# First product of an MLP behind an mLSTM cell: contraction of 320 rows in two full 128-row tiles and one 64-row pair, instead of five 64-row pairs

## Chip, core and metric

One core of a Trainium2 chip. The metric is the device time of one execution in microseconds. Before: median 490.5 us of 3 runs (490.28 to 491.42).

## What is computed

An mLSTM cell over 4 batches, 8 heads, 768 steps and head dimension 40, and a two-layer product with a leaky ReLU on its output, all in float32 (the weights `w_in` and `w_out` arrive as float64 and are narrowed on the chip):

```python
# per step t: C = f*C + i*(v k^T), n = f*n + i*k, with stabilised gates
h_tilde = C @ q;  denom = max(|n . q|, 1)
y = sigmoid(o_gate) * h_tilde / denom          # (4, 8, 768, 40)
x = y.transpose(0, 2, 1, 3).reshape(3072, 320) # heads side by side
h = x @ w_in                                   # 3072 x 320 x 2048, the first product
g = maximum(0.01 * h, h)
out = g @ w_out                                # 3072 x 2048 x 320
```

## The kernel before

The sequence is cut into six groups of 128 steps. A step `s` of the kernel is one batch of one group, so a group has four steps. For each step the cell is computed in chunked form by TensorE and DVE: scores (L593, L650), states (L608, L655), values (L673, L713, L743). The first group (steps 0 to 3) has a form of its own, the second another (`u_plain`), and steps from 8 on a third (`u_mix`).

The result of a step, `x` (128 tokens by 320), has to stand with its 320 columns on partitions before the first product can contract over them. For steps 0 to 7 DVE gates the values (`gate`, L685, or L724), GpSimd scales them by the denominators (`scale_x`, L702), TensorE transposes (`u_x`, L876 and L877) and ScalarE copies PSUM to `xT` (`x_copy`, L889 and L890). For later steps the transposed result goes through DRAM (`x_dr`, L762) and is gathered into `xT` by two requests of SyncE's queue (`gather_x`, L773).

The first product of a group, for its 512 tokens at once, makes 16 tiles of 128 hidden columns, two at a time (`j` = 0 to 7). The 320 contraction rows are five slots of 64. TensorE's array is split into two row tiles of 64 rows: row tile `r` = 0 works on one hidden tile and `r` = 1 on the other, beside each other, and both need all 64-row slots of `x`, so `xT` holds `x` twice, once on partitions 0 to 63 and once on 64 to 127, in 5 x 128 columns a step. `w_in` is held as four quarters of 512 hidden columns; on partitions 0 to 63 are the columns of `r` = 0, on 64 to 127 those of `r` = 1. Which row of `w_in` goes to which partition is free as long as `x` follows it.

Three kinds of first product exist. The first group runs in halves of 256 tokens (`half`), groups 1 to 3 in pairs of units of 512 (`pair`), both in fp32 (L907). Groups 4 and 5 split every operand into a rough part and rests and make three fp32r products (`three_units`, L833: "raw" and "low" into `ph`, "dif" into `pe`), which ScalarE and DVE join (L853, L855, L859). The splitting is done by DVE on `w_in` (in halves of 640 columns) and on `xT` (`split_x`, 640 columns a step). The second product follows in each group: plain in the first (L942, 128x320) and in seven block products afterwards (L983, 128x160).

`w_in` is loaded early by SyncE's queue (`load_weights`, "lw 0" to "lw 3" in the order below), ten requests a quarter (L230), each of 64 partitions by 256 float64. "nw" steps narrow a quarter to float32: ScalarE first (L260), then DVE (L262 to L277).

The order of work on PE, DVE, ScalarE and GpSimd is written out by hand, and each engine and queue takes its own in that order. For the first group it is a list (`ORDER`), of which these lines matter; afterwards units of products are interleaved with cell units by tables of places.

```python
ld 0; warm 12; ld 1; ld 2; lo 0; lo 1; lo 2; lw 0
g 0; ld 3; lw 1; lw 2; lo 3; ge 0; ug 0; tr 0 0
x 1; xc 1; gate 2; st 3; o 3; gp 2; nw 1; nw 1
stc 3; nw 1; ff 0; val 3; den 3; x 2; gate 3; fd 4
```

Here "ld" and "lo" are loads, "x" the transpose, "xc" the copy, "st" the state (L608), "ff" a unit of the first product. PSUM is two pools of four banks: `psf` ("mm") for the products, `psc` ("c") for cell work, transposes and `pe`.

Of the kernel before, what the change touches and what calls it, by code (L numbers as in the profile page):

```python
# [22 lines left out]
def kernel(  # L23
# [181 lines left out]
    def load_weights(n):  # L205

        m = n - QN
        if n < QN:
            dst = w_in[:, n, :]
        else:  # L210
            dst = w_out[:, 2 * m : 2 * m + 2, :].rearrange("p a d -> p (a d)")
        to = dst
        if wide:
            if n < 2:
                at = NF * GT - 2 * WC * (n + 1)
                raw = acts_l[:, at : at + 2 * WC].bitcast(U64)
            elif n < QN:
                raw = raw_t[:, WC * (n - 2) : WC * (n - 1)]
            elif m < 2:
                raw = w_out[:].rearrange("p f d -> p (f d)")[:, (2 + m) * WC : (3 + m) * WC].bitcast(U64)  # L220
            else:
                at = (4, 0, 1, 2, 3, 4)[m - 2] * HW
                raw = raw_t[:, at : at + HW]
            raws[n] = (raw, dst)
            to = raw
        if n < QN:
            src = moe_w_in[:, n * QC : (n + 1) * QC].rearrange("(p k) (r c) -> r p k c", p=DP, r=2)
            for slot in range(KC):
                for r in range(2):
                    nc.sync.dma_start(  # L230
                        to[DP * r : DP * (r + 1), 2 * P * slot : 2 * P * (slot + 1)], src[r, :, slot, :],
                    )
# [448 lines left out]
    def gate(s):  # L681

        d = st[s]
        d["x"] = cw.tile([P, Dm], F32, name="x")
        nc.vector.scalar_tensor_tensor(  # L685
            x_by(d["x"], H), in0=d["o"].rearrange("p (h a k) -> p h a k", h=H, k=KC), scalar=1.0,
            in1=d["pa"][:, :, :D].rearrange("p h (a k) -> p h a k", k=KC), op0=ALU.add, op1=ALU.mult,
        )

    def gate_scale(s):  # L690

        scale_x(st[s]["x"], st[s]["den"])

    def x_by(x, m):

        return x[:].rearrange("p (k m a) -> p m a k", k=KC, m=m)

    def scale_x(x, den):

        x4 = x[:].rearrange("p (k h a) -> p k h a", k=KC, h=H)  # L700
        by = den[:].unsqueeze(1).unsqueeze(3).to_broadcast([P, KC, H, DP // H])
        nc.gpsimd.tensor_tensor(x4, x4, by, op=ALU.mult)  # L702

    def u_plain(s):

        c, b = divmod(s, B)
        d = st[s]
        prep_o(s)
        hN = psc.tile([P, H, 2, V1], F32, name="hN", tag="c")
        m = mixed(s)  # L710
        for h in range(H):
            for u in range(2):
                nc.tensor.matmul(  # L713
                    hN[ts(u, SL), h].rearrange("p k d -> p (k d)"), lhsT=m[:, u, h, :], rhs=S_v[s % NL][:, u, h, :, :V1],
                    start=True, stop=True,
                )
        state_next(s, 1)
        den = cw.tile([P, H], F32, name="den")
        denominators(den[:], hN[:, :, 0, DB])
        if b < 2:  # L720
            d["x"] = cw.tile([P, Dm], F32, name="x")[:]
        else:
            d["x"] = wk.tile([P, H, D1], F32, name="hn")[:].rearrange("p h d -> p (h d)")[:, :Dm]
        nc.vector.scalar_tensor_tensor(  # L724
            x_by(d["x"], 2 * H), in0=natural(s, 2).rearrange("p h (k a i) -> p (h k) a i", k=2, i=KC), scalar=1.0,
            in1=hN[:].rearrange("p h k d -> p (h k) d")[:, :, :DB].rearrange("p n (a i) -> p n a i", i=KC),
            op0=ALU.add, op1=ALU.mult,
        )
        scale_x(d["x"], den)
        state_add(s, 1)  # L730

    def u_mix(s):
# [32 lines left out]
    def gather_x(s):  # L765

        c, b = divmod(s, B)
        if ("xT", c) not in st:
            st["xT", c] = wk.tile([P, B, KC * P], F32R if c in THREE else F32, name="xT", bufs=1)
        xT = st["xT", c][:].bitcast(F32)  # L770
        src = x_dr[s].rearrange("(m w) t -> m w t", w=QW)[:, :DB, :].rearrange("m (a k) t -> m a (k t)", k=KC)
# [7 lines left out]
    def open_parts():  # L779

        cells_stack.close()
        kp = ctx.enter_context(tc.tile_pool(name="kp", bufs=1))
        for key in ("raw", "low", "dif"):
            parts["w", key] = [kp.tile([P, WC], F32R, name=f"w_{key}{n}") for n in range(QN)]
        for key in ("low", "dif"):
            parts["x", key] = kp.tile([P, B, KC * P], F32R, name=f"x_{key}")
        parts["tmp"] = [kp.tile([P, KC * P], F32, name=f"tmp{n}") for n in range(2)]
        parts["n"] = 0

    def tmp_part():  # L790
# [10 lines left out]

    def split(src, low, dif):

        t = tmp_part()[:]
# [18 lines left out]
    def three_units(g, lead):  # L823

        xs = {"raw": by_slot(st["xT", g], F32R), "low": by_slot(parts["x", "low"], F32R), "dif": by_slot(parts["x", "dif"], F32R)}

        def rows(j, ph, key, start, stop):
            n, e = divmod(j, 2)
            for slot in range(KC):
                at = (2 * slot + e) * P  # L830
                for r in range(2):
                    part = slice(DP * r, DP * (r + 1))
                    nc.tensor.matmul(  # L833
                        ph[r][:], lhsT=parts["w", key][n][part, at : at + P], rhs=xs[key][part, slot, :],
                        start=start and slot == 0, stop=stop and slot == KC - 1,
                    )

        def triple(j):
            ph, pe = [], []

            def first():
                ph.extend(psf.tile([P, GT], F32, name=f"ph{r}", tag="mm") for r in range(2))
                rows(j, ph, "raw", True, False)

            def second():
                rows(j, ph, "low", False, True)

            def third():
                pe.extend(psc.tile([P, GT], F32, name=f"pe{r}", tag="c") for r in range(2))
                rows(j, pe, "dif", True, True)  # L850
# [19 lines left out]
    def u_x(s):  # L870

        c, b = divmod(s, B)
        d = st[s]
        xt = st["xt", s] = psc.tile([P, KF + 1, P], F32, name="xt", tag="c")
        for kk in range(KF):
            nc.tensor.transpose(xt[:, kk, :], d["x"][:, ts(kk, P)], ident[:])  # L876
        nc.tensor.transpose(xt[:KR, KF, :], d["x"][:, KF * P :], ident[:])  # L877
        del st[s]

    def x_copy(s):  # L880

        c, b = divmod(s, B)
        if b == 0:
            st["xT", c] = wk.tile([P, B, KC * P], F32, name="xT", bufs=1)
        xt = st.pop(("xt", s))
        xT = st["xT", c][:, b, :].rearrange("p (k t) -> p k t", t=P)
        for r in range(2):
            rows = ts(r, DP)
            nc.scalar.copy(xT[rows, 0::2, :], xt[:DP])  # L889
            nc.scalar.copy(xT[rows, 1::2, :], xt[DP:, :KF])  # L890

    def u_x1(s):
        u_x(s)
# [6 lines left out]
    def ff_units(g):  # L900
        xT = by_slot(st["xT", g])

        def rows(j, ph, cols, slots):
            bs = slice(cols.start // P, cols.stop // P)
            for slot in slots:
                for r in range(2):
                    nc.tensor.matmul(  # L907
                        ph[r][:, cols], lhsT=w_row(r, slot, j), rhs=xT[DP * r : DP * (r + 1), slot, bs, :],
                        start=(slot == 0), stop=(slot == KC - 1),
                    )  # L910

        def relu(j, ph, cols):
            for r in range(2):
# [3 lines left out]
        def pair(j):  # L917
            ph = []

            def first():  # L920
                ph.extend(psf.tile([P, GT], F32, name=f"ph{r}", tag="mm") for r in range(2))
                rows(j, ph, slice(0, GT), range(3))

            def second():
                rows(j, ph, slice(0, GT), range(3, KC))
                relu(j, ph, slice(0, GT))

            return [first, second]
# [1 line left out]
        def half(j, h):  # L930
            ph = [psf.tile([P, GT], F32, name=f"ph{r}", tag="mm") for r in range(2)]
            cols = slice(h * GT // 2, (h + 1) * GT // 2)
            rows(j, ph, cols, range(KC))
            relu(j, ph, cols)

        po = {}
# [393 lines left out]
```

## Time and profile before

| | |
|---|---|
| median of the runs | 490.5 us |
| profiled execution, span | 489.4 us |
| rest between the two | 1.1 us |
| TensorE busy | 476.1 us |
| first product, fp32 (L907) | 800 records, 146.3 us |
| first product, fp32r (L833) | 480 records, 63.4 us |
| second product (L942, L983) | 1248 records, 194.8 us |
| granted TensorE clock, mean | 0.982 |

Read the page's busy times for the engines, then the chain of work that ended last, then the waits of PE. An fp32 matmul stands in the trace as two records (two passes), an fp32r matmul as one. In a name such as "64*128" the first number is the rows and the second the columns of the array in use. Two records of row tiles that run beside each other overlap, so a group's busy time is smaller than its count times the mean. DMA requests that are being issued stand under "SPq".

### The profile page before, as it was taken

To read this page: it belongs to the slowest core of one execution; us is meant where nothing else is said; L and a number is where in the kernel's file an instruction comes from. 1 tells how busy PE (TensorE), PEld (TensorE's weight loads), DVE (VectorE), ACT (ScalarE), POOL (GpSimd) and SP (SyncE) were. 2 spreads that over 40 slices of the span, in tenths; PEclk is the share of its full clock that TensorE was granted. 3 is DMA by queue.
4 is the path that set the end of the run, shared out by engine and by line. 5 is a ranking of instruction groups with operands and counts; after the bars stand their busy time and mean duration, and the time that the engine had idled before them with its cause. 6 is when DMAs were issued, how large, how long until landed. Compare 5 with 4: busy or idle time off the path is not lost.

```text
span 489.4 us, 12856 instructions
## 1 busy us (share of the span) xinstructions
PE 476.1 (97%) x5137; PEld 377.9 (77%) x5137; DVE 365.9 (75%) x595; ACT 197.4 (40%) x510; POOL 160.3 (33%) x207
## 2 busy tenths in 40 slices
PE   7969998999999999999999999999999999999997
PEld 6857887777745479975559995557998889988997
DVE  5796999799924999777898777679899968335611
ACT  4674885453642240324342141425024752156310
POOL 4234454070600725817280563644220002100020
PEclk9867999999999999999999999999999999999999
DMA  7777686898623566668787877755151030100001
GB/s 136 177 191 146 161 226 134 216 229 177 143 97 90 133 158 176 162 152 202 152 197 160 189 181 177 184 144 153 44 229 42 1 107 1 42 15 0 1 1 54
DMA packets 142699, 63.41 MB, mean 130 GB/s; under 512 B 110832, under 2 KB 130864, under 8 KB 142640
## 3 DMA queue, kind: packets, MB, share of 16 engines
q1 hardware_dynamic: 142256, 62.47, 52.7%
q8 instruction: 40, 0.66, 0.6%
q14 instruction: 19, 0.16, 0.1%
q10 hardware_dynamic: 384, 0.13, 0.1%
HBM read 51.68 MB, written 8.27 MB: 122 GB/s over the span
## 4 chain that ended last, share of the span: by engine, by line
PE 82%; SPq 8%; DVE 5%; issue 2%; DMA 2%; ACT 1%; ACTq 0%; DVEq 0%
PE po L983 32%; PE ph L907 24%; PE ph L833 8%; PE po L942 6%; PE pe L833 4%; PE pT L743 3%; PE sd L650 3%; SPq L230 3%; SPq L368 2%; SPq L377 1%; PE sd L655 1%; DVE w_in L275 1%; PE hN L713 1%; DMA raw<-in_moe_w_in_dram 1%; DVE late L266 1%
## 5 line engine op out<-in xcount | busy, mean ns | idle before, releaser
L907 PE MATMUL ph<-xT,w_in 64*128 64x512 f32 (+1 forms) x800 | 146.3, 516 | 0.2 <-ACT xT L889 0.2
L907 PEld LDWEIGHTS ph<-xT,w_in 64*128 64x128 f32 x800 | 77.8, 190 | 57.4 <-issue 50.8
L983 PE MATMUL po<-w_out,acts 128*128 128x160 f32 x640 | 91.0, 301 | 0.0
L983 PEld LDWEIGHTS po<-w_out,acts 128*128 128x128 f32 x640 | 87.5, 190 | 3.4 <-ACT w L488 1.5
L915 ACT ACTIVATE acts<-ph 128x512 f32<-128x512 f32 (+1 forms) x80 | 36.8, 508 | 83.6 <-PE ph L907 83.5
L488 ACT ACTIVATE w<-w,gT 128x64 f32<-128x64 f32 (+1 forms) x192 | 52.0, 349 | 29.0 <-POOL w L480 28.0
L628 POOL TENSOR_TENSOR S<-S,f 40x336 f32<-40x336 f32 x36 | 32.5, 902 | 93.3 <-PE pT L743 49.5
L983 PE MATMUL po<-raw,acts 128*128 128x160 f32 x320 | 45.1, 299 | 0.0
L983 PEld LDWEIGHTS po<-raw,acts 128*128 128x128 f32 x320 | 44.0, 190 | 0.0
L660 DVE TENSOR_TENSOR qn<-w,sd 64x512 f32<-64x512 f32 x40 | 27.4, 684 | 21.0 <-PE sd L655 14.0
L1016 POOL TENSOR_TENSOR y<-y,raw 128x160 f32<-128x160 f32 x10 | 5.5, 555 | 112.3 <-ACT y L1015 112.3
L942 PE MATMUL po<-w_out,acts 128*128 128x320 f32 x128 | 36.0, 436 | 0.0
L855 DVE SCALAR_TENSOR_TENSOR acts<-ph,acts 128x512 f32<-128x512 f32 x32 | 20.6, 684 | 20.7 <-ACT acts L853 20.7
L541 DVE TENSOR_TENSOR qn<-kqT,late 64x512 f32<-64x512 f32 x32 | 33.1, 1033 | 1.0
L480 POOL TENSOR_TENSOR w<-w,i 128x512 f32<-128x512 f32 x20 | 31.8, 1591 | 2.7 <-ACT acts L915 1.9
L942 PEld LDWEIGHTS po<-w_out,acts 128*128 128x128 f32 x128 | 23.8, 190 | 9.5 <-issue 0.3
L757 POOL TENSOR_TENSOR xb<-xb,den 128x320 f32<-128x320 f32 x16 | 11.6, 727 | 48.7 <-DVE xb L754 48.7
L853 ACT ACTIVATE acts<-pe 128x512 f32<-128x512 f32 x32 | 17.4, 594 | 19.2 <-PE pe L833 19.0
L761 DVE STREAM_TRANSPOSE x<-xb 128x512 f32<-128x512 f32 x16 | 17.8, 1114 | 7.7 <-POOL xb L757 7.7
L859 ACT ACTIVATE acts<-acts 128x512 f32<-128x512 f32 x32 | 19.7, 633 | 8.0 <-DVE acts L855 8.0
L983 PE MATMUL po<-raw 128*128 128x160 f32 x160 | 22.7, 300 | 0.0
L650 PEld LDWEIGHTS sd<-kqT 40*64 40x64 f32 x640 | 19.7, 135 | 3.7 <-issue 3.0
(166 smaller groups left out, 773.2 us busy)
## 6 DMA issues: line engine op xcount, KB each, us to landing
w<-a_dr SPq DMA_DIRECT2D x40, 128.0 KB, 3.7
rb<-in_k_dram SPq DMA_DIRECT2D x64, 80.0 KB, 3.1
rb<-in_q_dram SPq DMA_DIRECT2D x64, 80.0 KB, 2.7
rb<-in_o_gate_dram SPq DMA_DIRECT2D x64, 80.0 KB, 2.6
xT<-x_dr SPq DMA_DIRECT2D x32, 160.0 KB, 3.2
late<-a_dr SPq DMA_DIRECT2D x32, 128.0 KB, 3.4
x_dr<-x SPq DMA_DIRECT2D x16, 256.0 KB, 3.4
kn<-in_k_dram SPq DMA_DIRECT2D x24, 160.0 KB, 3.7
```

Of the source, the lines that this page charges most:

```text
L480: nc.gpsimd.tensor_tensor(w, w, cm2.unsqueeze(1).to_broadcast([P, H, SL]), op=ALU.add)
L488: yield nc.scalar.activation(w[:, h, :], w[:, h, :], AF.Exp, bias=gT[c][:, 0, bh : bh + 1], scale=1.0)
L541: nc.vector.tensor_tensor(mixed(s)[rows, 1 - r], d["kqT"][rows, 1].rearrange("p (h t) -> p h t", t=SL), d["ea"][rows], op=ALU.mult,)
L628: nc.gpsimd.tensor_tensor(new, old, g, op=ALU.mult)
L650: nc.tensor.matmul(bank[1 - u][toks, h, :], lhsT=kqT[rows, 0, ts(h, SL)], rhs=kqT[rows, 1, ts(h, SL)], start=True, stop=True,)
L660: nc.vector.tensor_tensor(mixed(s)[toks, u], w[toks], bank[1 - u][toks], op=ALU.mult)
L833: nc.tensor.matmul(ph[r][:], lhsT=parts["w", key][n][part, at : at + P], rhs=xs[key][part, slot, :], start=start and slot == 0, stop=stop ...
L855: nc.vector.scalar_tensor_tensor(fs[r], in0=ph[r][:], scalar=1.0 + EPS, in1=fs[r], op0=ALU.mult, op1=ALU.add,)
L907: nc.tensor.matmul(ph[r][:, cols], lhsT=w_row(r, slot, j), rhs=xT[DP * r : DP * (r + 1), slot, bs, :], start=(slot == 0), stop=(slot == KC ...
L915: nc.scalar.activation(acts[:, f, cols], ph[r][:, cols], AF.Prelu, alpha=0.01)
L942: nc.tensor.matmul(po[n][:], lhsT=acts[:, f, ts(n, P)], rhs=w_out[:, f, :], start=(f == 0), stop=(f == NF - 1),)
L983: nc.tensor.matmul(bank[:], lhsT=left[:, f, :], rhs=right[:, f, :], start=f == 0, stop=f == KH - 1)
```

## The change

The 320 contraction rows are cut into 16 blocks of 20 rows. The first 16 rows of each block, 256 in all, form two slots of 128 rows (`MAIN`); the last 4 of each, 64 in all, stay a pair of 64-row tiles (`TAIL`). A hidden tile pair thus takes four full-row matmuls and one 64-row pair of matmuls per operand, in place of five pairs. Even `j` run the full-row part first and odd `j` the 64-row part, so that two neighbouring `j` meet in the same shape. In the triples the three operands are all run in one part before the other.

A quarter of `w_in` is loaded by three requests: 128 partitions by 2 rows of 512, and two of 64 partitions by 256. `xT` shrinks from 640 to 384 columns a step. The gather makes three requests. `gate` writes `x` in natural order and `scale_x` puts it into the new order in two operations with a tile of its own. The last 64 columns of `x` are transposed by two matmuls against the identity, one for each half of the partitions, and ScalarE copies all of it at once. `split_x` works on 384 columns.

```diff
+    KX = (KF + 1) * P
+    MB = 2 * H
-    def w_row(r, slot, j):
-        n, e = divmod(j, 2)
-        at = (2 * slot + e) * P
-        return w_in[DP * r : DP * (r + 1), n, at : at + P]
+    def col_of(r, slot, j):
+        e = j % 2
+        return KF * QC + e * P if slot == KF else slot * QC + (2 * r + e) * P
+    def rows_of(r, slot):
+        return slice(DP * r, DP * (r + 1)) if slot == KF else slice(0, P)
+    def w_tile(t, r, slot, j):
+        at = col_of(r, slot, j)
+        return t[rows_of(r, slot), at : at + P]
+    MAIN = [(r, slot) for r in range(2) for slot in range(KF)]
+    TAIL = [(r, KF) for r in range(2)]
+    def order_of(j):
+        return MAIN + TAIL if j % 2 == 0 else TAIL + MAIN
...
-            src = moe_w_in[:, n * QC : (n + 1) * QC].rearrange("(p k) (r c) -> r p k c", p=DP, r=2)
-            for slot in range(KC):
-                for r in range(2):
-                    nc.sync.dma_start(
-                        to[DP * r : DP * (r + 1), 2 * P * slot : 2 * P * (slot + 1)], src[r, :, slot, :],
-                    )
+            src = moe_w_in[:, n * QC : (n + 1) * QC].rearrange("(m w) c -> m w c", m=MB)
+            nc.sync.dma_start(
+                to[:, : KF * QC].rearrange("p (k c) -> p k c", k=KF),
+                src[:, : KF * DP // H, :].rearrange("m (a k) c -> m a k c", k=KF),
+            )
+            for r in range(2):
+                nc.sync.dma_start(to[DP * r : DP * (r + 1), KF * QC :], src[:, KF * DP // H :, 2 * P * r : 2 * P * (r + 1)])
...
+    def scale_x(dst, x, den):
+        x3 = x[:].rearrange("p (m w) -> p m w", w=DB)
+        src = x3[:, :, :TD].rearrange("p m (a k) -> p k m a", k=KF)
+        by = den[:].unsqueeze(1).unsqueeze(3).to_broadcast([P, KF, H, 2 * TD // KF])
+        nc.gpsimd.tensor_tensor(dst[:, : KF * P].rearrange("p (k m a) -> p k m a", k=KF, m=MB), src, by, op=ALU.mult)
+        by = den[:].unsqueeze(2).to_broadcast([P, H, 2 * (DB - TD)])
+        nc.gpsimd.tensor_tensor(dst[:, KF * P :].rearrange("p (m a) -> p m a", m=MB), x3[:, :, TD:], by, op=ALU.mult)
...
-        for r in range(2):
-            nc.sync.dma_start(xT[DP * r : DP * (r + 1), b, :], src)
+        nc.sync.dma_start(xT[:, b, : KF * P], src[:, : KF * DP // H, :].rearrange("m (a k) t -> m a (k t)", k=KF))
+        for r in range(2):
+            nc.sync.dma_start(xT[DP * r : DP * (r + 1), b, KF * P :], src[:, KF * DP // H : DB, :])
...
+            keys = ("raw", "low", "dif") if j % 2 == 0 else ("dif", "low", "raw")
+            half = [[(key, r, slot) for key in keys for r, slot in tiles] for tiles in (MAIN, TAIL)]
+            seq = half[0] + half[1] if j % 2 == 0 else half[1] + half[0]
...
-        nc.tensor.transpose(xt[:KR, KF, :], d["x"][:, KF * P :], ident[:])
+        for r in range(2):
+            nc.tensor.matmul(xt[ts(r, DP), KF, :], lhsT=d["x"][:, KF * P :], rhs=ident[:], start=True, stop=True)
...
-        for r in range(2):
-            rows = ts(r, DP)
-            nc.scalar.copy(xT[rows, 0::2, :], xt[:DP])
-            nc.scalar.copy(xT[rows, 1::2, :], xt[DP:, :KF])
+        nc.scalar.copy(st["xT", c][:, b, :].rearrange("p (k t) -> p k t", t=P), xt[:])
```

More of the change, by code (lines that the diff above doesn't have):

```diff
@@ L685, in gate @@
         nc.vector.scalar_tensor_tensor(
-            x_by(d["x"], H), in0=d["o"].rearrange("p (h a k) -> p h a k", h=H, k=KC), scalar=1.0,
-            in1=d["pa"][:, :, :D].rearrange("p h (a k) -> p h a k", k=KC), op0=ALU.add, op1=ALU.mult,
+            d["x"][:].rearrange("p (h d) -> p h d", d=D), in0=d["o"].rearrange("p (h d) -> p h d", d=D), scalar=1.0,
+            in1=d["pa"][:, :, :D], op0=ALU.add, op1=ALU.mult,
         )
     def gate_scale(s):
[L692 to L702, printed above, removed]
+        d = st[s]
+        x, d["x"] = d["x"], cw.tile([P, Dm], F32, name="xp")[:]
+        scale_x(d["x"], x, d["den"])
+    TD = KF * DP // H
+    def scale_x(dst, x, den):
[5 more added lines that the diff above has]
+        nc.gpsimd.tensor_tensor(dst[:, KF * P :].rearrange("p (m a) -> p m a", m=MB), x3[:, :, TD:], by, op=ALU.mult)
     def u_plain(s):
@@ L720, in u_plain @@
         if b < 2:
-            d["x"] = cw.tile([P, Dm], F32, name="x")[:]
+            d["x"] = cw.tile([P, Dm], F32, name="xp")[:]
         else:
             d["x"] = wk.tile([P, H, D1], F32, name="hn")[:].rearrange("p h d -> p (h d)")[:, :Dm]
+        x = cw.tile([P, Dm], F32, name="x")[:]
         nc.vector.scalar_tensor_tensor(
-            x_by(d["x"], 2 * H), in0=natural(s, 2).rearrange("p h (k a i) -> p (h k) a i", k=2, i=KC), scalar=1.0,
-            in1=hN[:].rearrange("p h k d -> p (h k) d")[:, :, :DB].rearrange("p n (a i) -> p n a i", i=KC),
-            op0=ALU.add, op1=ALU.mult,
+            x[:].rearrange("p (n d) -> p n d", d=DB), in0=natural(s, 2).rearrange("p h (k d) -> p (h k) d", k=2),
+            scalar=1.0, in1=hN[:].rearrange("p h k d -> p (h k) d")[:, :, :DB], op0=ALU.add, op1=ALU.mult,
         )
-        scale_x(d["x"], den)
+        scale_x(d["x"], x, den)
         state_add(s, 1)
@@ L785, in open_parts @@
         for key in ("low", "dif"):
-            parts["x", key] = kp.tile([P, B, KC * P], F32R, name=f"x_{key}")
-        parts["tmp"] = [kp.tile([P, KC * P], F32, name=f"tmp{n}") for n in range(2)]
+            parts["x", key] = kp.tile([P, B, KX], F32R, name=f"x_{key}")
+        parts["tmp"] = [kp.tile([P, WC // 2], F32, name=f"tmp{n}") for n in range(2)]
         parts["n"] = 0
@@ L802, in split @@
     def split(src, low, dif):
-        t = tmp_part()[:]
+        t = tmp_part()[:, : src.shape[1]]
         top_bits(t, src)
@@ L825, in three_units, with triple, target, rows @@
         xs = {"raw": by_slot(st["xT", g], F32R), "low": by_slot(parts["x", "low"], F32R), "dif": by_slot(parts["x", "dif"], F32R)}
[L827 to L830, printed above, removed]
-                for r in range(2):
-                    part = slice(DP * r, DP * (r + 1))
+        def triple(j):
+            bank = {}
+            keys = ("raw", "low", "dif") if j % 2 == 0 else ("dif", "low", "raw")
+            half = [[(key, r, slot) for key in keys for r, slot in tiles] for tiles in (MAIN, TAIL)]
+            seq = half[0] + half[1] if j % 2 == 0 else half[1] + half[0]
+            def target(it):
+                return "pe" if it[0] == "dif" else "ph", it[1]
+            def rows(todo):
+                for it in todo:
+                    key, r, slot = it
+                    mine = [other for other in seq if target(other) == target(it)]
+                    if it == mine[0]:
+                        pool, tag = (psc, "c") if key == "dif" else (psf, "mm")
+                        bank[target(it)] = pool.tile([P, GT], F32, name=f"{target(it)[0]}{r}", tag=tag)
                     nc.tensor.matmul(
-                        ph[r][:], lhsT=parts["w", key][n][part, at : at + P], rhs=xs[key][part, slot, :],
-                        start=start and slot == 0, stop=stop and slot == KC - 1,
-                    )
-        def triple(j):
-            ph, pe = [], []
+                        bank[target(it)][:], lhsT=w_tile(parts["w", key][j // 2], r, slot, j),
+                        rhs=xs[key][rows_of(r, slot), slot, :], start=it == mine[0], stop=it == mine[-1],
+                    )
             def first():
-                ph.extend(psf.tile([P, GT], F32, name=f"ph{r}", tag="mm") for r in range(2))
-                rows(j, ph, "raw", True, False)
+                rows(seq[:6])
             def second():
-                rows(j, ph, "low", False, True)
+                rows(seq[6:12])
             def third():
-                pe.extend(psc.tile([P, GT], F32, name=f"pe{r}", tag="c") for r in range(2))
-                rows(j, pe, "dif", True, True)
+                rows(seq[12:])
+                ph, pe = [[bank[key, r] for r in range(2)] for key in ("ph", "pe")]
                 fs = [acts[:, f_of(r, j), :] for r in range(2)]
@@ L883, in x_copy @@
         if b == 0:
[L884 removed]
+            st["xT", c] = wk.tile([P, B, KX], F32, name="xT", bufs=1)
         xt = st.pop(("xt", s))
[L886 to L890 removed]
+        nc.scalar.copy(st["xT", c][:, b, :].rearrange("p (k t) -> p k t", t=P), xt[:])
     def u_x1(s):
@@ L901, in ff_units, with rows @@
         xT = by_slot(st["xT", g])
-        def rows(j, ph, cols, slots):
+        def rows(j, ph, cols, todo):
             bs = slice(cols.start // P, cols.stop // P)
[L905 to L910, printed above, removed]
+            seq = order_of(j)
+            for at in todo:
+                r, slot = at
+                mine = [it for it in seq if it[0] == r]
+                nc.tensor.matmul(
+                    ph[r][:, cols], lhsT=w_tile(w_in[:, j // 2, :], r, slot, j), rhs=xT[rows_of(r, slot), slot, bs, :],
+                    start=at == mine[0], stop=at == mine[-1],
+                )
         def relu(j, ph, cols):
@@ L921, in first @@
                 ph.extend(psf.tile([P, GT], F32, name=f"ph{r}", tag="mm") for r in range(2))
-                rows(j, ph, slice(0, GT), range(3))
+                rows(j, ph, slice(0, GT), order_of(j)[:3])
             def second():
-                rows(j, ph, slice(0, GT), range(3, KC))
+                rows(j, ph, slice(0, GT), order_of(j)[3:])
                 relu(j, ph, slice(0, GT))
@@ L932, in half @@
             cols = slice(h * GT // 2, (h + 1) * GT // 2)
-            rows(j, ph, cols, range(KC))
+            rows(j, ph, cols, order_of(j))
             relu(j, ph, cols)
```

4 lines of the change are left out of this document (2 added, 2 removed).

## Prediction

> **What bounds the kernel now.** I read the page's busy times and its chain first.
>
> ```profile
> PE 476.1 (97%) x5137; PEld 377.9 (77%) x5137; DVE 365.9 (75%) x595; ACT 197.4 (40%) x510; POOL 160.3 (33%) x207
> PE 82%; SPq 8%; DVE 5%; issue 2%; DMA 2%; ACT 1%; ACTq 0%; DVEq 0%
> ```
>
> TensorE is busy 97% of the span. The chain leaves it only for SyncE's queue, DVE and DMA. PE's own waits say where those parts cost anything (columns: total us, times, longest).
>
> ```profile
> PE dC L608 <- ACT xT L890: 3.3, 1, 3.3
> PE warm L336 <- POOL ident masks.py:199: 1.5, 1, 1.5
> PE dC L608 <- POOL i L156: 1.4, 1, 1.4
> PE hN L713 <- DVE S L632: 1.0, 1, 1.0
> ```
>
> All of these fall before 80 us (the 3.3 us at 33.5 to 36.7, the 1.0 us just before 79.13). After that PE is the bound. The chain in order of time (start, us, what) shows its cost per piece.
>
> ```profile
> 120.58 4.50 PE po L942 x16
> 125.09 0.22 PE xt L876 x2
> 125.42 4.32 PE po L942 x16
> ...
> 186.97 19.76 PE po L983 x144
> 208.73 4.54 PE po L983 x32
> 215.29 13.07 PE ph L907 x60
> 230.38 4.49 PE ph L907 x20
> ...
> 430.30 1.13 PE pe L833 x10
> 431.43 2.32 PE ph L833 x20
> ```
>
> An fp32 matmul is two records in the trace. Two pieces of one kind with different counts give a slope and a rest:
> - L907, 64-row tiles, 512 columns: (13.07 - 4.49) / 40 = 0.2145 us a record, so 0.429 a pair of records. 20 records are 4.29 us; the rest, 4.49 - 4.29, is 0.20 us per stretch.
> - L983, all 128 rows, 160 columns: (19.76 - 4.54) / 112 = 0.136 a record; 32 are 4.35, rest 0.19.
> - L942, all rows, 320 columns: 4.32 / 16 = 0.270 a record in the second piece, whose neighbour before it is L876, another product in the same 128-row shape. The first piece, which follows L713 (64 output columns), costs 0.18 more.
>
> So each time PE changes the shape of its array tile, the new stretch costs 0.2 us; a change of product within one shape costs nothing.
>
> **The PE stream.** Per pair of output tiles the product has ten pair records of 512 columns now. The change makes eight full-row records and two pair records. The full-row price at 512 columns is not in the trace; from 160 and 320 columns it is 0.270 + 192 x (0.270 - 0.136) / 160 = 0.431 (an estimate), against 0.429 for a pair. Five units stay five units: no gain in fp32. The 256-column halves of the first group go the same way. Fewer weight loads (ten become six) save nothing, since they are already beside matmuls.
>
> **The fp32r products (L833).** A pair takes 1.13 / 5 = 0.226 to 2.32 / 10 = 0.232, about 0.23 us for one pass of 512 columns, where half an fp32 pair is 0.2145. No row shows a full-row fp32r matmul. The nearest row by type and columns is L833 itself, so I take 0.23 and no gain. If the excess belongs to paired rows, the low end is 0.216: 16 pairs of tiles x 12 records = 192 records x 0.014 = 2.7 us less. If 128 rows of fp32r read more slowly by as much again as the excess now, the high end is 2.7 us more.
>
> **Shape changes.** In the order of the built instructions (no time is in it) the stretches of equal tile shape go from 14 to 27 between the first L907 and 79.13 us, and from 59 to 101 after it. The latter 42 are: 44 inner changes (4 halves, 24 fp32 pairs, 16 triples, each changing once inside), plus 8 because four transposes of `x` (L877, one 64-column transpose in the 128-row shape) become two matmuls that write 64 partitions each and return, less 10 at the ends of products, which now begin and end in full rows beside L942 and L983. A 64-column stretch costs less: L743 and L713, 2.02 us for 64 and 1.06 for 32 records, leave 0.10 us each. So 38 x 0.20 + 4 x 0.10 = 8.0 us after 79 us, all on PE's path. The four extra transposing matmuls add a second pass of 128 columns, about 0.11 us each by L876 (0.22 for two): 0.4 us. Before 79 us: 11 x 0.20 + 2 x 0.10 = 2.4 us.
>
> The Trainium skill's page "TensorEngine Tiling (Array Packing)", section "Key Properties", says that changing the tiling mode, not just the tile, drains TensorE. It names no figure; it speaks against this change and leaves the rival "free inside a product" below without ground, to which I still give a little.
>
> **The x copies.** Four ScalarE copies per step (0.47, 0.37, 0.47, 0.37 us) become one of 128x384, 0.47 by the same row. Before the second group's first product PE waits 0.2 us on the last of them, and its first 60 records take 14.01 us (from 135.24), where those from 215.29 take 13.07. Of these 1.1 us I take 0.6 back, since ScalarE's copies of L942's results stay ahead in its queue. GpSimd scales in two operations instead of one (0.83 us becomes some 0.7 + 0.25): eight times, under PE's work except before the first four transposes. DVE's gate writes contiguously, 0.68 to at least 0.49 us (L754, same size): off the path.
>
> **The requests.** SyncE's queue issues ten requests per w_in quarter.
>
> ```profile
> 12.97 7.66 SPq L230 DMA_DIRECT2D acts<-in_moe_w_in_dram  x10
> 24.55 6.50 SPq L230 DMA_DIRECT2D acts<-in_moe_w_in_dram  x10
> 33.55 1.35 ACT L260 ACTIVATE late<-acts 128x1280 bf16<-128x1280 bf16 x1 [2.02 <-DMA raw<-in_moe_w_in_dram]
> ```
>
> Seven fewer at 0.65 us are 4.5 us per quarter, for whatever stands behind: step 3's loads, the second quarter, the gates. The bytes stay (1.3 MB a quarter); 128 KB requests land 2.9 us after issue, the 640 KB of w_out 6.4. So between no earlier at all and 9 us earlier for the second quarter; I take about 5, enough for what follows. ScalarE stops at 31.5 us for the second quarter, and behind that wait stand the x copies that free the PSUM bank for L608. Without it: ACT is at L260 by 30.3 (the first x copy takes 0.5, not 1.7), done 31.7; the second transpose on PE ends near 33.7 in the slow clock; copy to 34.3; L608 at 34.35 instead of 36.71. That is 2.35 us. The first product needs the first narrowed quarter, which DVE ends at 34.5: not late. PE then carries 2.4 us of shape changes and 0.2 of transposes to L713, whose free arrival is 77.88 - 2.35 - 0.25 (a q load that lands sooner) + 2.6 = 77.9, while DVE, which shifts with it, is ready at about 76.8. So L713 goes from 79.13 to 77.9: 1.2 us earlier. Ends: 0.8 us later if no transfer comes sooner and the changes all show, 3.9 us earlier if PE's 2.35, 0.25 and 1.26 us of waits all go and the changes hide in DVE's time.
>
> The gather of `x` has three requests per step instead of two, 16 more at 0.6 us on SyncE's queue. It runs from the last product unit of the group before, 30 us ahead of its reader, and moves 196 KB instead of 320: nothing. `split_x` on 384 instead of 640 columns takes some 0.3 us from each of 24 DVE operations, in a stage where no PE wait names DVE: nothing.
>
> **Sum.** After 79 us: 8.0 + 0.4 - 0.6 = 7.8 slower. Before: 1.2 faster. fp32r: 0. Net 6.6. The profiled span is 489.4 us; the median of the runs is 490.5, 1.1 more, which I keep: 497.1, say 497.0.
>
> **Rivals.**
> - Faster by the start (0.06). From 20 to 42 us PE is busy 18.2 us at a granted clock of 0.51 to 0.67. If the early weights close PE's gaps and the clock returns at 30 instead of 42 us, 7 us of it go, on top of 3.9: 490.5 + 7.8 - 10.9 = 487.4. It decides from a start more than 7.8 us shorter. Against: DVE is busy 4.90 of 5 us and 7.16 of 7.4 in that time, so it holds L608 and the first product back.
> - Shape changes free inside a product (0.04): 490.5 - 3.9 - 0.2 = 486.4, down to 484 with fp32r's 2.7. Against: L907 to L983 costs 0.2, L942 to L876 nothing.
> - The parts nearly cancel (0.06): start 3.9, fp32r 2.7 and changes at two thirds, 490.5 + 5.2 - 6.6 = 489 to 492.
> - A weight load for all rows can't run beside a matmul in the same rows (0.02): L673, 41 columns, is paced by its loads at 7.9 / 64 = 0.12 us. After 79 us there are 4 x 8 + 24 x 8 + 192 = 416 full-row records: 50 us, time 547. Against: L983's 0.136 us a record is its 160 columns, with a load under each one. The Trainium skill's page "TensorE: Matmul & The Clock Gate", section "The mechanism", says that loads overlap matmuls in flight only where the row group differs; its other rule there, a background buffer, fits this trace, and L983 decides for it.
> - A new wait in the fp32r stage (0.06): a triple now holds both its `pe` banks for all of its 3.45 us, not for 1.13. ScalarE needs 2 x 0.59 + 2 x 0.63 = 2.4 us a triple and DVE 1.4, so two triples' banks should do; if not, a microsecond per triple, 16 us, 513.
> - The forecast: 0.76.
>
> **Chances and range.** Faster by over 0.3% (1.5 us, about what a measurement can tell from no change): 0.06 + 0.04 + 0.01 of the cancelling case = 0.11. Within: 0.05. Slower: 0.76 + 0.06 + 0.02 = 0.84. The forecast's ends are 497.1 - 2.7 (start) - 2.7 (fp32r) = 491.7 and 497.1 + 2.0 + 2.7 = 501.8. Both extremes at once are unlikely: 492.3 to 501.0 holds the forecast and most of the cancelling case.
>
> **What would show it.** Right: full-row records of the first product at 0.43 us in fp32, a rest of 0.2 us at every change between 128 and 64 rows, stretches lengthened by some 8 us from 79 us on, the 3.3 us wait at L608 mostly gone, no new PE waits after 80 us. The fp32r triples now take 3.45 us; they should take 3.65. Wrong: changes without a rest, full-row records much over 0.43, a PE wait in the fp32r stage, or first products starting before 33 us.

## The result, and the profile after

| | before | after |
|---|---|---|
| median of the runs | 490.96 us (490.28 to 492.04, 4 runs) | 497.68 us (497.07 to 497.99, 4 runs) |
| ratio after / before | | 1.0138, 95% interval 1.0112 to 1.0164 |
| profiled execution, span | 489.4 us | 495.5 us |
| granted TensorE clock, mean | 0.982 | 0.986 |

The change makes the kernel slower by 1.4%, which is 6.8 us, between 5.5 and 8.1. The forecast was 497.0 us.

In the changed kernel the first product is L934 (fp32) and L865 (fp32r), the second L969 and L1010, the state L626, the transposes L904 and L906, GpSimd's scaling L721 and L723. The page's busy times and its chain, for the kernel after:

```profile
PE 486.0 (98%) x4649; PEld 373.1 (75%) x4649; DVE 358.6 (72%) x595; ACT 186.7 (38%) x486; POOL 167.4 (34%) x215
...
PE 95%; POOL 2%; DVE 2%; issue 1%; DVEq 0%; POOLq 0%
```

PE has 488 records fewer than before (4649 for 5137) and is busy 9.9 us longer. ScalarE and DVE lost 10.7 and 7.3 us of work, and the time did not follow them. SyncE's queue, 8% of the chain before, is gone from it, and PE took its place. PE's waits after (total us, times, longest):

```profile
PE dC L626 <- POOL vu L520: 2.1, 1, 2.1
PE warm L354 <- POOL ident masks.py:199: 1.5, 1, 1.5
PE dC L626 <- DVE w L618: 1.4, 1, 1.4
PE tkq L596 <- DVE w L618: 0.8, 1, 0.8
PE xt L906 <- POOL xp L723: 0.5, 1, 0.5
```

The reader is to see two things. Nothing here falls after 80 us, so from there on the time is PE's own stream. And the 3.3 us that the state waited for ScalarE are gone, but 2.1 us for GpSimd stand in their place.

The chain in order of time, after (start, us, what):

```profile
136.23 13.47 PE ph L934 x36
...
188.21 19.76 PE po L1010 x144
...
216.54 13.67 PE ph L934 x36
...
232.22 4.69 PE ph L934 x12
```

The pieces answer to those of before one by one. A pair of hidden tiles is 12 records now, of which 8 are full-row and 4 run as two pairs; it was 20, run as ten pairs. Three pairs of tiles took 13.07 us and take 13.67; one took 4.49 and takes 4.69. With ten units of 0.429 us a pair of tiles is 4.29 us: 4.69 - 4.29 = 0.40, two shape changes of 0.20, and 13.67 - 12.87 = 0.80, four of them. The first piece begins in full rows behind L969, which has that shape too, and holds three: 13.47. The second product's 144 records take 19.76 us in both kernels.

Where the 0.2 us lies can be read from TensorE's weight loads (PEld) around one full-row part, its 64-row part and the next full-row part. The brackets give the engine's idle time before a load.

```profile
219.15 0.19 PEld L934 LDWEIGHTS ph<-xT,w_in 128*128 128x128 f32 x1 [0.24 <-issue]
220.09 0.30 PEld L934 LDWEIGHTS ph<-xT,w_in 64*128 64x128 f32 x4 [0.76 <-issue]
220.63 0.19 PEld L934 LDWEIGHTS ph<-xT,w_in 64*128 64x128 f32 x2 [0.24 <-DVE den L683]
...
222.01 0.30 PEld L934 LDWEIGHTS ph<-xT,w_in 128*128 128x128 f32 x2 [0.76 <-issue]
```

Within a shape the next weights are loaded beside the running matmul, one load every 0.429 us. The load at 219.15 is for the last full-row record, which starts at 219.57; without a change the next record would start at 220.00. The first load of the new shape begins only at 220.09, together with its matmul, and the record after it starts 0.53 later instead of 0.43. The delays of 0.09 and 0.10 make the 0.2: at a change the first weights are not loaded ahead.

The window of two fp32r triples, after:

```profile
375.89 0.67 PE ph L865 x4
376.56 0.47 PE pe L865 x4
377.02 0.46 PE ph L865 x4
377.48 1.11 PE pe L865 x4
378.59 3.70 PE ph L865 x16
382.29 0.91 PE pe L865 x4
```

From 375.89 to the end of the last piece at 383.20 are 7.31 us for two triples, 3.65 each, where one took 3.45. The two shape changes of the pair of triples sit in the first piece and in the fourth.

By stage, each from the start of its first matmul to that of the next stage, in us (before, after): second product of the first group 43.05, 44.12; first product of groups 1 to 3 42.05, 42.56, then 39.65, 41.14, then 42.06, 43.45; of groups 4 and 5 27.85, 29.33 and 27.82, 29.34; the four second products between them each 0.10 to 0.31 shorter, the last 0.22. From the second `hN` (79.13 us before, 78.17 after) on, the stages add up to 7.0 us more.

### The profile page after: what moved, and what is told of

The parts are those of the page before. It is cut to its first block, busy times and chain, and to the rows that moved or that the text cites. A ratio compares the mean times of both kernels' runs of the same rounds, so it can differ in the third digit from the quotient of the medians.

```text
span 495.5 us, 11842 instructions
## 1 busy us (share of the span) xinstructions
PE 486.0 (98%) x4649; PEld 373.1 (75%) x4649; DVE 358.6 (72%) x595; ACT 186.7 (38%) x486; POOL 167.4 (34%) x215
## 4 chain that ended last, share of the span: by engine, by line
PE 95%; POOL 2%; DVE 2%; issue 1%; DVEq 0%; POOLq 0%
PE po L1010 31%; PE ph L934 30%; PE ph L865 8%; PE po L969 7%; PE pe L865 4%; PE pT L764 3%; PE sd L668 3%; PE pa L691 1%; PE sd L673 1%; PE warm L354 1%; PE hN L734 1%; PE tk L582 1%; PE tq L568 1%; PE sc L611 1%; POOL xp L723 1%; PE tg L365 1%
## 5 line engine op out<-in xcount | busy, mean ns | idle before, releaser
L934 PE MATMUL ph<-xT,w_in 128*128 128x512 f32 (+3 forms) x480 | 152.3, 528 | 0.0
L934 PEld LDWEIGHTS ph<-xT,w_in 128*128 128x128 f32 (+1 forms) x480 | 72.5, 190 | 68.5 <-issue 63.5
L1010 PE MATMUL po<-w_out,acts 128*128 128x160 f32 x640 | 90.4, 300 | 0.0
L1010 PEld LDWEIGHTS po<-w_out,acts 128*128 128x128 f32 x640 | 87.9, 190 | 2.1 <-issue 1.2
L942 ACT ACTIVATE acts<-ph 128x512 f32<-128x512 f32 (+1 forms) x80 | 38.2, 508 | 90.8 <-PE ph L934 90.5
L1010 PE MATMUL po<-raw,acts 128*128 128x160 f32 x320 | 45.1, 299 | 0.0
L1010 PEld LDWEIGHTS po<-raw,acts 128*128 128x128 f32 x320 | 44.0, 190 | 0.0
L969 PE MATMUL po<-w_out,acts 128*128 128x320 f32 x128 | 36.2, 437 | 0.0
L969 PEld LDWEIGHTS po<-w_out,acts 128*128 128x128 f32 x128 | 23.8, 190 | 9.7 <-issue 0.3
L865 PE MATMUL ph<-xT,w_raw 128*128 128x512 f32 (+1 forms) x96 | 23.9, 413 | 0.0
L865 PE MATMUL ph<-x_low,w_low 128*128 128x512 f32 (+1 forms) x96 | 23.6, 391 | 0.0
L1062 DVE TENSOR_TENSOR hn<-hn,po 128x160 f32<-128x160 f32 x10 | 3.2, 320 | 27.4 <-issue 14.2
```

Source lines behind the costliest of these rows:

```text
L865: nc.tensor.matmul(bank[target(it)][:], lhsT=w_tile(parts["w", key][j // 2], r, slot, j), rhs=xs[key][rows_of(r, slot), slot, :], start=it ...
L934: nc.tensor.matmul(ph[r][:, cols], lhsT=w_tile(w_in[:, j // 2, :], r, slot, j), rhs=xT[rows_of(r, slot), slot, bs, :], start=at == mine[0] ...
L942: nc.scalar.activation(acts[:, f, cols], ph[r][:, cols], AF.Prelu, alpha=0.01)
L969: nc.tensor.matmul(po[n][:], lhsT=acts[:, f, ts(n, P)], rhs=w_out[:, f, :], start=(f == 0), stop=(f == NF - 1),)
L1010: nc.tensor.matmul(bank[:], lhsT=left[:, f, :], rhs=right[:, f, :], start=f == 0, stop=f == KH - 1)
```

## The experiments

The theory: PE bounds the kernel from 80 us on; full rows bring no rate; each change between the 128-row and the 64-row shape costs 0.2 us; the requests only touch the start. The rivals: full-row records differ from pairs by themselves; changes are free and something else was added; the requests carry the gain or the loss. The ratios below are to runs of the kernel before that were taken beside each, with their 95% intervals. Stages behind about 92 us repeat between kernels to 0.01 us where the code is the same and PE waits for nothing new, so single profiles tell hundredths there (the last stage, which ends with the final output, only tenths); the start does not repeat like that (the granted clock between 30 and 36 us was 0.64 in one execution and 1.00 in another), and differences of a microsecond or two before 92 us are read from medians only.

### The requests alone, in the kernel before

```diff
-            for slot in range(KC):
-                for r in range(2):
-                    nc.sync.dma_start(
-                        to[DP * r : DP * (r + 1), 2 * P * slot : 2 * P * (slot + 1)], src[r, :, slot, :],
-                    )
+            for r in range(2):
+                nc.sync.dma_start(to[DP * r : DP * (r + 1), :].rearrange("p (k c) -> p k c", k=KC), src[r])
```

> The kernel before with a quarter of w_in in two requests (64 partitions by 5 rows of 256 columns each) instead of ten; the product is untouched. Theory (the time is lost to changes of tile shape on PE, the requests only buy a little at the start): ScalarE no longer waits 2.0 us for the second quarter, L608 starts some 2 us earlier than 36.71, the stages from 80 us on keep their lengths, and the time falls by 0.5 to 2.5 us, to about 489. Rival (the requests were the chain of the start and all of the waits before 80 us are theirs): 3.9 us or more faster. Rival (larger requests hold up what is queued behind them): no gain or a loss.

Measured: 490.99 us, ratio 1.0004 [0.9990, 1.0018]. The 0.5 to 2.5 us that were expected did not come, and the rival of larger requests that hold up what is queued behind them is the one that fits. SyncE's queue in that run (start, us, line):

```profile
12.68 1.43 SPq L229 DMA_DIRECT2D acts<-in_moe_w_in_dram  x2
14.15 0.60 SPq L365 DMA_DIRECT2D kn<-in_k_dram  x1
14.80 1.73 SPq L365 DMA_DIRECT2D qn<-in_q_dram  x1
16.58 5.92 SPq L365 DMA_DIRECT2D S<-in_v_dram  x1
22.54 2.35 SPq L229 DMA_DIRECT2D acts<-in_moe_w_in_dram  x2
```

The quarter is issued in 1.43 us instead of 7.66, as meant. But of the loads behind it that of `v` then takes 5.92 us to issue, 2.57 before, and the second quarter starts only 2 us sooner (22.54 against 24.55). The DMA engines' mean busy share between 20 and 30 us went from 0.75 to 0.94. The state still waited 2.6 us for ScalarE's copy of `xT`, instead of 3.3. These two requests cover 64 partitions each, where the change has one of 128 and two of 64, so the run is near to the change's requests and not the same.

### The product alone: after, with ten requests a quarter

```diff
-            nc.sync.dma_start(
-                to[:, : KF * QC].rearrange("p (k c) -> p k c", k=KF),
-                src[:, : KF * DP // H, :].rearrange("m (a k) c -> m a k c", k=KF),
-            )
+            rows = src[:, : KF * DP // H, :].rearrange("m (a k) c -> k m a c", k=KF)
+            for slot in range(KF):
+                for half in range(2):
+                    for r in range(2):
+                        at = slot * QC + 2 * P * half
+                        nc.sync.dma_start(
+                            to[DP * r : DP * (r + 1), at : at + 2 * P],
+                            rows[slot, H * r : H * (r + 1), :, 2 * P * half : 2 * P * (half + 1)],
+                        )
```

> The changed kernel with its first product, gather and transposes, but with a quarter of w_in in ten requests of 64 partitions by 256 columns, as before. Theory: the stages from 80 us on are those of the changed kernel, 7 us longer than before; the start loses what the three requests bought, so about 1 us more than the changed kernel, 498 to 499.5. Rival (the slower time comes from the new requests): back to 491.

Measured: 500.39 us, ratio 1.0183 [1.0162, 1.0203], 0.9 us above the expected 498 to 499.5. From 95 us on the stages are those of the changed kernel to 0.01 us, but for the last (33.75 for 33.64). So the product costs 9.0 us (8.0 to 10.0), and three requests give back some 2.2 us of it (1.0183 - 1.0138). The two intervals meet at 1.016, so the size of 2.2 is rough. It lies ahead of 95 us, and among PE's waits the one of the kernel before is back (L631 is the state, L920 the copy):

```profile
PE dC L631 <- ACT xT L920: 3.3, 1, 3.3
```

The changed kernel waits 2.1 us for GpSimd there. In the kernel before, two requests a quarter in place of ten were worth nothing. Why fewer requests help the one start and not the other, no run settles.

### One 128-row matmul, and one 64-row matmul, in each pair of the kernel before

The matmul adds zeros to 32 columns. It is the same in both kernels but for its rows, and stands between slots 2 and 3, at the head of `second()`, in each of the 24 pairs of hidden tiles of groups 1 to 3.

```diff
+                nc.tensor.matmul(
+                    ph[0][:, :32], lhsT=zeros[:128].to_broadcast([128, P]), rhs=xT[:128, 0, 0, :32],
+                    start=False, stop=False,
+                )
```

(with `zeros[:64]`, `[64, P]` and `xT[:64, ...]` in the other).

> The kernel before with one matmul more in each of the 24 fp32 pairs of groups 1 to 3: zeros over 128 rows times 32 columns of x, added to the first bank between the two units, so the result is the same. It takes PE from the 64-row shape to the 128-row shape and back. Theory: two records of about 0.11 us (paced by weight loads) and two changes of shape of 0.2 us, 0.6 us a pair, 24 pairs: 15 us more, 505.5. Rival (a change costs nothing inside a product): 5 us more or less, as in the run with 64 rows.

> The same with zeros over 64 rows, so that the extra matmul keeps the 64-row shape. Theory: only its two records, 0.06 to 0.22 us a pair, 1.5 to 5.5 us more, 492 to 496; the difference to the run with 128 rows is 24 x 0.4 = 9.6 us, between 8 and 13. Rival: no difference between the two.

Measured: 504.30 us, 1.0268 [1.0245, 1.0290], with 128 rows; 495.87 us, 1.0100 [1.0083, 1.0117], with 64. The chain of the first (start, us, what; L925 is the added matmul):

```profile
141.97 0.34 PE ph L925 x2
142.31 4.49 PE ph L907 x20
146.80 0.34 PE ph L925 x2
```

and of the second:

```profile
142.10 0.11 PE ph L925
142.21 4.40 PE ph L907 x20
146.61 0.11 PE ph L925
```

The period with 128 rows is 4.83 us (146.80 - 141.97), with 64 rows 4.51, without either 4.29. With 128 rows the 20 records behind the added matmul show the rest of 0.20 (4.49), and the matmul itself takes 0.34 where the 64-row one takes 0.11: if its own work is the 0.11 of the 64-row one, the two changes are 0.20 and 0.23. But the 64-row matmul costs 0.22 us a pair and not the 0.11 of its record, since the 20 records behind it also take 0.11 more than 4.29; with all of that taken off, the two changes together are 0.32. So this pair of runs gives 0.16 to 0.21 us for a change. Over 24 pairs the chains differ by 7.7 us and the medians by 8.4, where 9.6 were expected for 48 changes of 0.20. The medians hold more than the matmuls: both runs also have a wait of PE for a load of `q` that the kernel before has not (1.0 and 1.4 us), and their first fp32r stage took 28.49 and 28.80 us for 27.85. That the lone row tile of the 64-row matmul holds up the pairing of the next is likely, and no run shows it.

### No alternation of the order

```diff
-        return MAIN + TAIL if j % 2 == 0 else TAIL + MAIN
+        return MAIN + TAIL
...
-            seq = half[0] + half[1] if j % 2 == 0 else half[1] + half[0]
+            seq = half[0] + half[1]
```

> The changed kernel with the full-row part always first, for odd j too: no two neighbouring tile pairs meet in one shape. The same matmuls; in the order of the built instructions 193 stretches of equal shape instead of 149, 37 of the 44 more after 79 us. Theory: 37 x 0.2 = 7.4 us more than the changed kernel, and up to 1.4 before 79 us: 505 to 506.5. Rival (the loss is the price of the full-row matmuls themselves or of something else that is in both): 497.7.

Measured: 507.29 us, ratio 1.0350 [1.0319, 1.0381], 9.6 us above after by the medians and 10.4 by the ratios, and 0.8 above the upper end of what was expected. Three and four pairs of tiles in that run's chain:

```profile
243.00 18.76 PE ph L934 x48
...
329.39 14.07 PE ph L934 x36
```

18.76 - 4 x 4.29 = 1.60, eight changes in four pairs; 14.07 - 12.87 = 1.20, six in three, where the alternating order has four. The fp32r stages went from 29.33 and 29.34 to 30.96 each, 1.63 us for eight more changes. The profile has 7.2 us more from 92 us on, where 7.4 were expected; the rest of its 8.9, 1.7 us, lies in the start, where up to 1.4 was. Free changes would have left 497.7.

### The old transpose of the last 64 columns

```diff
-        for r in range(2):
-            nc.tensor.matmul(xt[ts(r, DP), KF, :], lhsT=d["x"][:, KF * P :], rhs=ident[:], start=True, stop=True)
+        nc.tensor.transpose(xt[:KR, KF, :], d["x"][:, KF * P :], ident[:])
...
-        nc.scalar.copy(st["xT", c][:, b, :].rearrange("p (k t) -> p k t", t=P), xt[:])
+        xT = st["xT", c][:, b, :].rearrange("p (k t) -> p k t", t=P)
+        nc.scalar.copy(xT[:, :KF, :], xt[:, :KF, :])
+        for r in range(2):
+            nc.scalar.copy(xT[ts(r, DP), KF, :], xt[:DP, KF, :])
```

> The changed kernel with the last 64 columns of x transposed as before, once, to 64 partitions in the 128-row shape, and three copies by ScalarE instead of one. Theory: four visits to the 64-column shape after 79 us go, 0.3 us each with the stretch behind them, and four second passes of 0.11: 1.6 us less, 496.1; the start unchanged within 1 us. Rival (those transposes lie beside other work): no difference.

Measured: 496.54 us, ratio 1.0121 [1.0093, 1.0149]. By the medians 1.1 us less than after, which the intervals do not tell apart; the stage does. One step's transposes in the chain of after:

```profile
124.52 0.22 PE xt L904 x2
124.74 0.37 PE xt L906 x4
125.11 4.50 PE po L969 x16
```

and of this kernel, where L905 is the old transpose and L971 the second product:

```profile
125.79 0.22 PE xt L904 x2
126.01 0.11 PE xt L905
126.12 4.31 PE po L971 x16
```

The two matmuls that write 64 partitions each cost 0.26 us more than the one transpose, and the product behind them 0.19 more: 0.45 a step. The stage took 42.35 us for 44.12, 1.77 less, where 1.6 was expected.

### Full rows without the 64-row part

```diff
-        return MAIN + TAIL if j % 2 == 0 else TAIL + MAIN
+        return MAIN
...
-            seq = half[0] + half[1] if j % 2 == 0 else half[1] + half[0]
+            seq = half[0]
```

> The changed kernel without the 64-row part: the last 64 contraction rows are left out of the first product in all groups. No change of shape inside a product is left. Theory: in groups 1 to 3 each pair of tiles loses four records (0.86 us) and one change (0.2), 1.06 x 24 = 25.4; in groups 4 and 5 three passes of 0.23 and one change, 0.89 x 16 = 14.2; in the first group 0.63 a half, some 10 in all, part of it hidden by DVE before 79 us: 40 to 49 us less, about 451. The stages of groups 2 to 5 show it without the start: an fp32 pair 3.43 us, a triple 2.76. Rival (changes cost nothing inside a product): 0.2 us less gain per pair and triple, 8 us less gain from group 1 on.

This kernel leaves out 64 of the 320 rows and so no longer computes the product; only its times are of use. Measured: 470.98 us, ratio 0.9610 [0.9584, 0.9636]. The expectation of 451 us was missed by 20. What the run was for, the price of a full row, stands in its chain without any change of shape inside a piece:

```profile
134.71 10.30 PE ph L934 x24
...
426.34 1.82 PE pe L865 x8
428.16 3.70 PE ph L865 x16
```

10.30 / 24 = 0.429 us for a full-row fp32 record of 512 columns, and 0.228 to 0.231 for fp32r. In group 5, where PE is still the bound, the stage fell by 7.18 us, from 29.34 to 22.16; 8 x 0.89 = 7.1 was the theory, 5.5 the rival with free changes. Up to the first group's second product its profile is only 1.8 us shorter than after's (90.14 for 91.95), where some 10 were expected; the granted clock there was 0.50 between 30 and 36 us, for 1.00 in the profile of after. From there on it is 24.7 us shorter, where 39.6 were expected. Where that part went is on its page and among its PE waits:

```profile
PE 447.7 (95%) x4393; PEld 358.7 (76%) x4393; DVE 358.1 (76%) x595; ACT 186.7 (40%) x486; POOL 170.5 (36%) x215
...
PE 59%; DVE 13%; DMA 9%; POOL 8%; SPq 4%; issue 3%; ACT 2%; ACTq 0%; POOLq 0%; DVEq 0%
```

```profile
PE sd L673 <- POOL vu L526: 4.7, 3, 1.9
PE po L1010 <- ACT acts L942: 1.9, 2, 1.1
PE ph L934 <- ACT acts L942: 1.6, 2, 1.0
```

PE's busy time fell by 38.3 us, but its idle time rose from 9.5 to 21.3, behind the cells' DVE and GpSimd work and ScalarE's evictions. So PE is the only bound of the changed kernel from 80 us on, but not by far: 38 us of PE work taken away shortened the time by 27.

## Why the prediction was right, and where its terms were off

- **Full rows bring no rate in fp32.** Right: 0.431 was worked out from 160 and 320 columns, 0.429 measured, the same as a pair.
- **fp32r at 0.23 us in either shape.** Right: 0.228 to 0.231. Neither end of the 2.7 us bracket came true.
- **Shape changes.** Right in kind, and in size to a twentieth: 7.0 us from 79 us on, less 0.4 for the extra transposing matmuls and with the 1.1 of the next point added back, leave 7.7 for the changes, where 8.0 stood. The rival of free changes is refuted by the pieces of after and the order without alternation (0.20 a change each), by the 128-row zero matmul (0.16 to 0.21), and by the transposes, whose visit to the 64-column shape cost 0.34 a step beside the 0.11 of the second pass, where 0.3 was taken.
- **The x copies.** The term was too small. 0.6 us was taken back and all of the 1.1 came: the first 60 records took 14.01 us where 13.07 was the price, and now that piece shows no lost time (13.47, three pairs and three changes); the wait of 0.2 before it is gone too.
- **The start.** The size looks near in the two profiles, 0.96 us earlier at the second `hN` (L713, now L734) for 1.2, but the start doesn't repeat that well. By the medians the kernel is 6.7 us slower, the stages from 79 us on give 7.0, and the time outside the span fell by some 0.2 us, so the start gained about 0.1 us, give or take 1.3. And the step to it failed. L608 was to go from 36.71 to 34.35; L626 starts at 35.93. ScalarE's wait for the second quarter did fall, from 2.02 to 0.33 us. The term that was mis-sized is GpSimd's second scaling operation, priced at 0.25. In the first group it took 1.54, and the next memset (L164, 0.93 for 0.25 elsewhere) and L516 and L520 behind it were stretched as well. GpSimd in that stretch of after:

```profile
29.40 1.54 POOL L723 TENSOR_TENSOR xp<-x,den 128x64 f32<-128x64 f32 x1
...
32.78 1.66 POOL L516 TENSOR_TENSOR vu<-S,gT 128x320 f32<-128x320 f32 x1
34.41 1.47 POOL L520 TENSOR_TENSOR vu<-S,gT 128x16 f32<-128x16 f32 x1
```

and DVE in it:

```profile
29.00 1.79 DVE L284 SCALAR_TENSOR_TENSOR late<-acts,late 128x1280 uint16<-128x1280 uint16 x1
...
32.37 1.49 DVE L293 SCALAR_TENSOR_TENSOR w_in<-acts,w_in 128x1280 f32<-128x1280 uint32 x1
33.90 1.90 DVE L295 SCALAR_TENSOR_TENSOR w_in<-w_in,late 128x1280 f32<-128x1280 f32 x1
```

L723 ends at 30.94, 0.15 us after DVE's L284; L520, 16 columns, ends at 35.88, 0.08 after L295; L516 ends 0.58 after L293. L723's shortest execution in the same trace is 0.30 us, and L516 and L520 took 0.72 and 0.23 at 25.4 and 26.1. Two further executions of L723, at 44.80 and 64.81, took 1.54 and 1.55, and each ended 0.16 after a two-input operation of DVE. The Trainium skill's page "SBUF — State Buffer", section "SBUF: two separate sides", says that DVE and GpSimd share one pair of ports, and that of an operation of DVE with two SBUF inputs and a GpSimd operation that reads SBUF the one that starts first holds the pair for its whole length while the other is blocked. The coincidences agree with it: DVE's operation was the first to start in each, and L295, which starts while L516 still runs, took 1.90 us for 1.49 elsewhere. No run here moved one of the operations away to test it. Two inputs are not the only case. The memset ended 0.19 after DVE's L289, which reads one tensor, and the kernel before had a sign of it: its L502, 16 columns as well, took 0.80 us at 30.01 and ended 0.08 after the one-input L271.

- **The requests.** Their share in that start was overrated. Fewer requests alone were worth nothing; beside the new product three give back about 2.2 us. The Trainium skill's page "DMA: Bandwidth & Descriptors", section "Rules for kernel authors", advises one transfer over 128 partitions in place of two over disjoint halves. The gain of three requests over ten in the changed kernel is on its side; the ratio of 1.0004 for two half transfers instead of ten requests shows how little the count matters while the bytes in front stay.
- **What lies outside the span.** The 1.1 us that the prediction kept is not a rest of one execution: it sets the median of the runs against the span of a longer one. Within one execution the rest is 1.84 to 2.11 us in 28 later runs of the kernel before, and 1.74 to 1.91 in the four after. So the span of 489.4 belongs to a run some 0.9 us above the median, and the 6.1 us between the two profiles are too little by about as much. The medians grew by 6.7, where the sum had 6.6. That it is this near is in part luck: the start gave less than was taken, and the copies more. The forecast ends 0.7 below the median, 0.5 of it because the median of the kernel before rose from 490.5 to 490.96 with a fourth run.
- **The other rivals.** No PE wait appeared in the fp32r stage, so two triples' `pe` banks do suffice. Full-row loads are hidden at 0.429 us a record within one shape, which ends the 547 us case. The start did not shorten by 7.8 us, and the parts did not cancel to 489 to 492.

## What to carry to other kernels

Packing a short contraction into fuller array tiles gained nothing here, since the row tiles already ran beside each other: count units of array time and not matmuls, and then count how often the shape changes, at about 0.2 us each in this kernel. Where changes can't be avoided, let neighbours meet in the same shape; the alternation was worth 9 to 10 us here. And before a leaner transfer or a shorter operation is credited, ask what the same consumer waits for next.

## What the runs showed of the hardware that was not expected

- A change between the 128-row and the 64-row shape cost 0.2 us, and the first weights of the new shape were not loaded ahead: their load began with the matmul itself, 0.52 us after the matmul before, where 0.43 is the pace within a shape.
- A GpSimd operation of 128x64 took 0.30 us at its shortest and 1.55 at its longest in one trace, the three above 1 us beside DVE operations with two inputs in SBUF.
- Larger requests did not free SyncE's queue in step with their number: the issue of the load of `v` behind them took 5.62 us in the changed kernel and 5.92 in the first experiment, for 2.57 before, with the DMA engines' busy share at 0.93 and 0.94 between 20 and 30 us.
- The granted clock at the start differs between executions: between 30 and 36 us it was 0.64 in the profile of the kernel before and 1.00 in that of the one with 64-row zeros, whose code is the same up to there; it was 1.00 in that of the kernel after and 0.50 in that of the run without its 64-row part.
